# A causal attention and gated FFN kernel: another order and other transfers at its start

## Chip, cores, metric

The kernel runs on one core of a Trainium2 chip. The metric is the time of one execution on the device in microseconds. Runs of one kernel are compared by their median; beside them stands one execution that was recorded by the hardware profiler, from which all durations of single instructions come.

## What is computed

Eight batches of eight heads, 576 positions, head width 64, in float32; then a gated feed-forward block over all 4608 rows of width 512. Cut to what matters:

```python
scores = (q @ k.T) / sqrt(64)                  # per batch and head
cum    = cumsum(max(s, 0), axis=-1)
bias   = -(cum[:, None] - cum[None, :])
scores = where(causal, -1e9, scores + minimum(bias, 0))
attn   = softmax(scores)
x      = concat_heads(attn @ v)                # 4608 x 512
out    = (silu(x @ w_gate) * (x @ w_val)) @ w_out
```

## The kernel before

The kernel schedules every instruction by hand: the order in which the program calls its helpers is the order of each engine's queue. Heads are taken in groups of four ("batches" of the program, `hb`); batch 0 holds heads 0 to 3, batch 1 heads 4 to 7, and together they are the first of the eight batches of the reference. In a group, head `hh` belongs to row half `r = hh // 2` and column half `e = hh % 2`.

**The operand tiles.** `KQ[i][r]` holds, for the groups of parity `i`, 128 partitions: 64 carry the transposed k and q of two heads, side by side in the columns, and of the other 64 four carry the bias terms; the rest are zero. For `r = 0` the bias terms are in partitions 64 to 67. A score piece (`score_piece`, matmuls L373) multiplies a 128-column block of the k side with columns of the q side; the bias comes out of the same product, since the four extra rows hold the running sum of s, split into a high and a low bf16 part, and constants. Heads of the first batch add the causal mask by a matmul with the tile `lower` (L367). ScalarE takes the exponential of each piece (L383) and gives the PSUM bank back. A head has four pieces.

**The running sum.** VectorE scales s (L240), sums it in one scan (L241), rounds the sum to bf16 (L244), subtracts to get the low part (L245) and copies both parts (L246) in the tile `HL`. For head 0 the rows are made on chip: `pick` multiplies `HL` with a selecting matrix (L914; the high part is `lo` = 0, the low part `lo` = 1), and `picked_row` scales and shifts the product from PSUM into `KQ[0][0]`, for one side on ScalarE (L925), for the other on VectorE (L929). All other heads get their rows by `aug`, a DMA from `HL` for each head (L188).

**k and q of batch 0** are loaded in four quarters (k and q, row halves 0 and 1) by SP, in float32; ScalarE casts the first two to bf16 (L268), GpSimd the other two (L270). TensorE transposes each (`row_half`, L315) and the result is copied out of PSUM into `KQ` by `pe_out` (L328 on ScalarE, L330 on VectorE).

**Batch 1** is loaded by GpSimd's queue (L145). VectorE casts k (L260), GpSimd casts q (L260). `half_batch` transposes a whole k or q on TensorE (L301) and copies out row half 0; the copies of row half 1 come later, after the scores of head 3, and only they give the PSUM banks back (L330; four copies for each row half).

**V** is loaded in five chunks by GpSimd's queue (L162), cast by GpSimd (four) and VectorE (the fifth), L173. `init_vt` sets the column of ones beside each head's V and zeroes the padding.

**PSUM** has eight banks. `take` gives the bank that was released longest ago in the order of the program, so a bank's next user waits for its last reader, whichever engine that is.

**The order at the start.** TensorE first runs 32 matmuls on the identity (`keep_warm`, L900) while the first loads are under way. Then come row half 0 of batch 0, the picks, head 0 (with row half 1 transposed in between), head 1, the transposes of k 1, the first two pieces of head 2, the transposes of q 1, the rest of head 2, head 3, heads 4 and 5, and after them the first values products (`values(0, 1)`, L410). The feed-forward block (L643, L749 and others) begins some microseconds later and then runs interleaved with the attention of the next batches to the end.

Of the kernel before, what the change touches and what calls it, by code (L numbers as in the profile page):

```python
# [13 lines left out]
BF16 = mybir.dt.bfloat16  # L14
AF = mybir.ActivationFunctionType
ALU = mybir.AluOpType
# [3 lines left out]
def kernel(  # L20
# [89 lines left out]
    r_m = first.tile([128, 1], FP32)  # L110
    PTP = {0: first, "bufs": 7}
    lower = first.tile([128, 512], BF16)

    with tc.manual_schedule():
        loaded = {}
# [19 lines left out]
        def view(b, w):  # L135
            return bank[b][:, 0:w]
# [4 lines left out]
        def load_one(hb, name, rs=(0, NR), eng=nc.sync):  # L141
            b, g = divmod(hb, 2)
            if rs[0] == 0:
                loaded[name, hb] = raw.tile([128, NR, J, D], FP32, tag="raw" + name, name="raw" + name)
            eng.dma_start(  # L145
                loaded[name, hb][:, rs[0] : rs[1], :, :].rearrange("x r j d -> x r (j d)"),
                SRC[name][0][b, g * HB + 2 * rs[0] : g * HB + 2 * rs[1], :, :].rearrange(
                    "(r e) (p j) d -> (e p) r (j d)", e=2, j=J
                ),
            )  # L150

# [42 lines left out]
        def init_vt(i):  # L194
            nc.gpsimd.memset(VT[i][:, :, :, D : D + 1], 1.0)
            nc.gpsimd.memset(VT[i][64:128, 4, :, 0:D], 0.0)

        for r in range(NR):
            load_one(0, "k", (r, r + 1))
            load_one(0, "q", (r, r + 1))  # L200

        nc.vector.memset(warm, 0.0)
        nc.vector.memset(one_s, 1.0)
        nc.scalar.activation(warm, warm, AF.Exp)
        nc.vector.memset(sel, 0.0)
        nc.vector.memset(HL[:, 0:2, 0, :].bitcast(FP32), ONES2)
        nc.vector.memset(HL[:, 2:4, 1, :].bitcast(FP32), NEGS2)
        make_identity(nc, ident)
        nc.gpsimd.memset(lower, 0.0)
        nc.gpsimd.affine_select(  # L210
            lower, lower, pattern=[[0, 4], [1, 128]],
            compare_op=ALU.is_ge, fill=nc.gpsimd.to_reg(MASKED), base=0, channel_multiplier=-1,
        )
# [8 lines left out]
        nc.vector.memset(aug_rows(0, 0)[:, :, S // 2 :], 0.0)  # L222

        def pads(i):
            for r in range(2):
                nc.gpsimd.memset(KQ[i][r][64 * r : 64 * r + 64, :, NR * S :], 0.0)

        for i in range(2):
            rows = aug_rows(i, 1)
# [1 line left out]
                rows.rearrange("p a n -> p (a n)"),  # L231
                one_s[0:64, 0:1].to_broadcast([64, NR * S + 64]), 0.0,
            )
        nc.gpsimd.memset(aug_rows(1, 0), 0.0)
        pads(0)
        pads(1)
        for nm in ("k", "q"):
            load_one(1, nm, eng=nc.gpsimd)

        nc.vector.tensor_scalar(s_sb, s_sb, 0.0, 8.0, ALU.max, ALU.mult)  # L240
        nc.vector.tensor_tensor_scan(  # L241
            c8, one_s[0:BH, 0:1].to_broadcast([BH, S]), s_sb, 0.0, ALU.mult, ALU.add
        )
        nc.vector.tensor_copy(HL[:, 0, 1, :], c8)  # L244
        nc.vector.tensor_sub(HL[:, 1, 1, :], c8, HL[:, 0, 1, :])  # L245
        nc.vector.tensor_copy(HL[:, 2:4, 0, :], HL[:, 0:2, 1, :])  # L246

        SP4 = [nc.sync] * 4
        GP4 = [nc.gpsimd] * 4

        cts = {}

        def cast_one(hb, name, eng):
            cts[name, hb] = cp.tile([128, J, NR, D], BF16, tag="c" + name, bufs=2, name="c" + name)
            dst = cts[name, hb].rearrange("x j r d -> x r j d")
            src_t = loaded[name, hb]
            if eng is nc.scalar:
                nc.scalar.copy(dst, src_t)
            else:
                eng.tensor_copy(dst, src_t)  # L260

        def cast_half(hb, name, r, eng):
            if r == 0:
                cts[name, hb] = cp.tile([128, J, NR, D], BF16, tag="c" + name, bufs=2, name="c" + name)
            dst = cts[name, hb][:, :, r, :]
            src_t = loaded[name, hb][:, r, :, :]
            if eng is nc.scalar:
                nc.scalar.copy(dst, src_t)  # L268
            else:
                eng.tensor_copy(dst, src_t)  # L270
# [35 lines left out]
        def pe_transpose_half(hb, name, g, r):  # L306
            j0, j1 = JG[g]
            if r == 0:
                bs = EARLY[name][g]
                ps = view16(bs, (j1 - j0) * 128).rearrange("p (j x) -> p j x", x=128)  # L310
                tps[name, g] = [ps, bs, 2]
            ps = tps[name, g][0]
            ct = cts[name, hb]
            for j in range(j0, j1):
                nc.tensor.transpose(  # L315
                    ps[64 * r : 64 * r + 64, j - j0, :], ct[:, j, r, :], ident
                )

        def pe_out(hb, name, g, r, eng):
# [32 lines left out]
        def score_piece(bh, ci):  # L352
            hb, hh = divmod(bh, HB)
            masked = bh < H
            if ci == 0:
                pts[bh] = PTP[0].tile(
                    [128, PTW], BF16, tag="pt", bufs=PTP["bufs"], name="pt"
                )
            pt = pts[bh]
            r, e = divmod(hh, 2)  # L360
            T = KQ[hb % 2][r]
            bs = take()
            n = sum(hi - lo for _, lo, hi in CHUNKS[ci])
            sc = view(bs, n)
            masked_here = masked and ci in (0, 3)
            if masked_here:
                nc.tensor.matmul(  # L367
                    sc, ident, lower[:, 0:n], start=True, stop=False, skip_group_check=True
                )
            o = 0  # L370
            for (tj, lo, hi) in CHUNKS[ci]:
                w = hi - lo
                nc.tensor.matmul(  # L373
                    sc[:, o : o + w],
                    T[:, 1, e * S + 128 * tj : e * S + 128 * (tj + 1)],
                    T[:, 0, e * S + lo : e * S + hi],
                    start=not masked_here,
                    stop=True,
                    skip_group_check=masked_here,
                )  # L380
                o += w
            c0 = CHUNK_PT[ci]
            nc.scalar.activation(pt[:, c0 : c0 + n], sc, AF.Exp, scale=0.125)  # L383
# [513 lines left out]

        def keep_warm(n, b):
            for _ in range(n):
                nc.tensor.matmul(view(b, 128), ident, ident, start=True, stop=True)  # L900

        def row_half(nm, r):
            for g in range(2):
# [3 lines left out]
            for g in range(2):  # L907
                pe_out(0, nm, g, r, engs[g])

        def pick(side):  # L910
            b = PICK[side]
            for lo in range(2):
                for c0, c1 in ((0, 512), (512, S)):
                    nc.tensor.matmul(  # L914
                        banks[:, b + c0 // 512, 0 : c1 - c0], sel[:, lo, :],
                        HL[:, lo, 1, c0:c1], start=(lo == 0), stop=(lo == 1),
                        skip_group_check=True,
                    )

        def picked_row(side):  # L920
            b = PICK[side]
# [24 lines left out]
                av_piece(h, range(NCH))  # L946
                av_out(h)

        keep_warm(32, 7)
        cast_half(0, "k", 0, nc.scalar)  # L950
        cast_half(0, "q", 0, nc.scalar)
        aug(0, SP4, range(1, HB))
        aug(1, SP4)
        row_half("k", 0)
        row_out("k", 0, nc.scalar, nc.scalar)
        cast_half(0, "k", 1, nc.gpsimd)
        cast_half(0, "q", 1, nc.gpsimd)
        load_v(0, range(5), nc.gpsimd)
        row_half("q", 0)
        pick(1)  # L960
        pick(0)
        pe_out(0, "q", 0, 0, nc.scalar)
        pe_out(0, "q", 1, 0, nc.vector)
        picked_row(1)
        picked_row(0)
        row_half("k", 1)
        score_piece(0, 0)
        score_piece(0, 1)
        row_half("q", 1)
        row_out("k", 1, nc.vector, nc.vector)  # L970
        cast_one(1, "k", nc.vector)
        row_out("q", 1, nc.vector, nc.vector)
        score_piece(0, 2)
        score_piece(0, 3)
# [146 lines left out]
```

## Time and profile before

| | |
|---|---|
| median of 3 runs | 374.61 us (373.37 to 375.18) |
| profiled execution | 373.92 us, its span 372.0 us |
| granted TensorE clock, mean | 0.998 |
| TensorE busy | 363.2 us (98%) in 3288 matmuls |
| VectorE busy | 291.1 us (78%) |
| ScalarE busy | 239.9 us (65%) |
| GpSimd busy | 212.4 us (57%) |
| DMA | 64.21 MB, mean 173 GB/s |

The span runs from the first to the last instruction that the profiler recorded; the execution is longer by what lies around it. "Busy" does not count instructions that issue a DMA. In the lists of the trace, lines of the form "start, duration, engine, line, operation, output<-input, shapes, count" merge neighbouring instructions of one line, and a bracket tells how long the engine had been idle and what ended that. "DVE" is VectorE, "ACT" ScalarE, "PE" TensorE, "POOL" GpSimd; "PEld" is TensorE's weight load.

### The profile page before, as it was taken

What the parts mean: (1) busy time and instruction counts of PE and PEld (TensorE: products, weight loads), DVE (VectorE), ACT (ScalarE), POOL (GpSimd) and SP (SyncE); (2) the same over time, 40 slices, a digit from 0 to 9 for tenths busy, and PEclk for the clock granted to TensorE, in tenths of its full rate; (3) what the DMA queues carried; (4) which work ended last, traced back from release to release, by engine and by line L of the source; (5) the groups of instructions that cost most, each with busy time, mean ns of one, the idle gap of its engine ahead of it and who ended that gap; (6) DMA issues with size and microseconds to landing.
All of it is one profiled execution on the core that took longest, in us unless ns stands there. A gap on an engine that the chain in (4) does not pass through costs nothing.

```text
span 372.0 us, 8786 instructions
## 1 busy us (share of the span) xinstructions
PE 363.2 (98%) x3288; PEld 230.3 (62%) x3288; DVE 291.1 (78%) x585; ACT 239.9 (65%) x470; POOL 212.4 (57%) x325
## 2 busy tenths in 40 slices
PE   7899999999999999999999999999999999999996
PEld 6684556655555557855685558655865585476465
DVE  8978776377985899589967897699868867975984
ACT  8877776778886967688757875786565523323321
POOL 8983556955266547594749464955675516315320
PEclk9999999999999999999999999999999999999999
DMA  7999999799879996996789484994142113002003
GB/s 238 220 254 259 215 272 257 239 299 227 252 172 307 199 268 181 162 285 217 214 179 263 160 185 157 265 210 114 40 121 62 35 30 118 0 3 86 28 0 113
DMA packets 97133, 64.21 MB, mean 173 GB/s; under 512 B 77228, under 2 KB 82724, under 8 KB 97092
## 3 DMA queue, kind: packets, MB, share of 16 engines
q1 hardware_dynamic: 84964, 41.46, 46.9%
q0 software_dynamic: 12128, 22.21, 22.7%
q8 instruction: 25, 0.41, 0.5%
q14 instruction: 16, 0.13, 0.1%
HBM read 37.90 MB, written 19.86 MB: 155 GB/s over the span
## 4 chain that ended last, share of the span: by engine, by line
PE 83%; DVE 10%; DMA 2%; ACT 2%; issue 2%; POOL 1%; DVEq 0%; ACTq 0%
PE banks L643 43%; PE banks L749 17%; PE banks L373 9%; PE banks L410 7%; PE banks L700 5%; DVE kq L330 3%; DMA pk<-ks 2%; DVE pp L666 2%; DVE ht L677 1%; DVE kq L288 1%; ACT th L664 1%; POOL vt L173 1%; ACT pt L383 1%; PE banks L459 1%; PE banks L301 0%
## 5 line engine op out<-in xcount | busy, mean ns | idle before, releaser
L383 ACT ACTIVATE pt<-banks 128x512 bf16<-128x512 f32 (+1 forms) x256 | 120.4, 511 | 29.8 <-PE banks L373 17.1
L643 PE MATMUL banks<-XT,wg 128*128 128x512 bf16 x432 | 111.4, 379 | 0.4 <-DVE pp L666 0.3
L643 PE MATMUL banks<-XT,wv 128*128 128x512 bf16 x432 | 110.9, 379 | 0.1
L664 ACT ACTIVATE th<-banks 128x512 bf16<-128x512 f32 x108 | 64.7, 599 | 56.3 <-PE banks L643 51.4
L666 DVE SCALAR_TENSOR_TENSOR pp<-th,banks 128x512 bf16<-128x512 bf16 x108 | 73.7, 682 | 18.3 <-ACT th L664 18.0
L677 DVE SCALAR_TENSOR_TENSOR ht<-pp,banks 128x512 bf16<-128x512 bf16 x108 | 74.1, 687 | 10.3
L373 PE MATMUL banks<-kq 128*128 128x128 bf16 (+4 forms) x576 | 76.4, 240 | 0.8 <-DVE kq L330 0.3
L686 POOL TENSOR_TENSOR ht<-ht 128x512 bf16<-128x512 bf16 x35 | 40.4, 1154 | 53.3 <-DVE su L684 53.2
L373 PEld LDWEIGHTS <-kq 128*128 128x128 bf16 x576 | 46.1, 98 | 30.7 <-issue 2.4
L643 PEld LDWEIGHTS <-wv 128*128 128x128 bf16 x432 | 38.4, 98 | 36.2 <-issue 0.2
L643 PEld LDWEIGHTS <-wg 128*128 128x128 bf16 x432 | 38.4, 98 | 34.1 <-issue 0.7
L410 PEld LDWEIGHTS <-pt 128*128 128x128 bf16 x960 | 41.8, 98 | 17.7 <-issue 0.7
L388 POOL TENSOR_SCALAR_AFFINE_SELECT pt<-pt 128x512 bf16<-128x512 bf16 x56 | 36.6, 653 | 25.9 <-ACT pt L383 21.7
L410 PE MATMUL banks<-vt,pt 128*128 128x65 bf16 x960 | 46.8, 194 | 0.5 <-DVE ot L427 0.4
L444 POOL DMA_DIRECT2D xs<-ot x24 | 21.7, 904 | 30.4 <-DVE ot L427 28.0
L749 PEld LDWEIGHTS <-ht 128*128 128x128 bf16 x336 | 31.2, 98 | 4.3
L427 DVE TENSOR_TENSOR ot<-banks,rc 128x320 bf16<-128x320 f32 x64 | 31.5, 492 | 2.2
L188 POOL DMA_DIRECT2D kq<-HL x48 | 29.2, 610 | 0.0
L700 PE MATMUL banks<-wo,ht 128*128 128x512 bf16 x96 | 25.8, 379 | 0.0
L749 PEld LDWEIGHTS <-su 128*128 128x128 bf16 x252 | 23.6, 98 | 3.3
L814 POOL TENSOR_TENSOR ysb<-ysb 128x512 f32<-128x512 f32 x12 | 15.2, 1269 | 15.3 <-DVE ysb L808 15.3
L749 PE MATMUL banks<-WS,ht 128*128 128x256 bf16 x168 | 22.9, 273 | 0.0
(101 smaller groups left out, 377.2 us busy)
## 6 DMA issues: line engine op xcount, KB each, us to landing
out_dram<-ysb POOLq DMA_DIRECT2D x32, 256.0 KB, 4.0
rawv<-in_v_dram SPq DMA_DIRECT2D x28, 256.0 KB
rawk<-in_k_dram SPq DMA_DIRECT2D x12, 576.0 KB
rawq<-in_q_dram SPq DMA_DIRECT2D x12, 576.0 KB
xs<-ot POOLq DMA_DIRECT2D x24, 160.0 KB, 3.7
ks<-ck SPq DMA_DIRECT2D x11, 288.0 KB
qs<-cq SPq DMA_DIRECT2D x11, 288.0 KB
rawk<-in_k_dram POOLq DMA_DIRECT2D x3, 576.0 KB, 6.0
```

Of the source, the lines that this page charges most:

```text
L373: nc.tensor.matmul(sc[:, o : o + w], T[:, 1, e * S + 128 * tj : e * S + 128 * (tj + 1)], T[:, 0, e * S + lo : e * S + hi], start=not maske ...
L383: nc.scalar.activation(pt[:, c0 : c0 + n], sc, AF.Exp, scale=0.125)
L388: nc.gpsimd.affine_select(pt[:, 1088:1600], pt[:, 1088:1600], pattern=[[0, 4], [1, 128]], compare_op=ALU.is_ge, fill=zreg, base=0, channel ...
L410: nc.tensor.matmul(av[:, bi * (D + 1) : (bi + 1) * (D + 1)], pt[:, c0 : c0 + 128], VT[b % 2][:, tj, h, :], start=(tj == 0), stop=(tj == bi),)
L427: nc.vector.tensor_mul(ot[:, :, e * D : (e + 1) * D], av3[:, :, 0:D], rc[:, :, None].to_broadcast([128, NCH, D]),)
L643: nc.tensor.matmul(view(bs, TT), w[:, c, f0 : f0 + 128], xt[:, c, :], start=(c == 0), stop=(c == 3),)
L664: nc.scalar.activation(th, pg, AF.Tanh, scale=0.5)
L666: nc.vector.scalar_tensor_tensor(pp, in0=th, scalar=1.0, in1=pg, op0=ALU.add, op1=ALU.mult)
L677: nc.vector.scalar_tensor_tensor(hp[:, 2 * k2 : 2 * k2 + 2, :].rearrange("p a n -> p (a n)"), in0=pp, scalar=0.5, in1=pv, op0=ALU.mult, op ...
L686: (nc.vector if ft == NFT - 1 else nc.gpsimd).tensor_sub(hp[:, 1:3, :], hp[:, 1:4:2, :], hp[:, 0:3:2, :])
L700: nc.tensor.matmul(view(pys[ts_], DM), hps[ft // 2][:, 2 * (ft % 2) + half, c0 : c0 + 128], WO[j][:, ft % WKO, :], start=(ft == 0), stop=( ...
L749: nc.tensor.matmul(ps, lhs(p), rhs(p), start=(first and p == 0), stop=(last and p == NP - 1), skip_group_check=True,)
```

## The change

All of it lies in the first 20 us, but for the number of partitions in the scores of row half 0, which holds for all batches.

1. The four quarters of k and q of batch 0 are loaded by GpSimd's queue, which casts them to bf16 on the way (`load_first`); the four casts on ScalarE and GpSimd are gone, `cast_half` with them. The identity is made ahead of these loads, the mask tile `lower` behind them. k of batch 1 is loaded next, q of batch 1 only after `lower`, the zeroed pads and V's ones (`init_vt(0)`, which moves to this place).
2. The scan of s, its rounding and the subtraction run in two halves of 288 columns; ScalarE rounds the first half. The copy of both parts (L246) becomes `second_copy`, behind the bias rows of head 0.
3. Head 1's rows are written by three DMAs from `HL`, the low and high part straight from where they are made (`aug_one`); heads 2 and 3 get theirs as before, after `second_copy`.
4. Scores of row half 0 read 68 partitions instead of 128. The zeroing of the other partitions (L222 on VectorE, L234 on GpSimd) is gone.
5. The picks run high parts first, then low parts.
6. q of batch 1 is cast by VectorE instead of GpSimd.
7. The transposes of k 1 come after the first two pieces of head 2, those of q 1 after its last two.
8. `keep_warm` multiplies a zeroed tile `idle` instead of the identity, 31 times instead of 32, and 18 more such matmuls stand between head 0's third and fourth piece, on a bank of their own.

The diff's core:

```diff
+        def load_first(name, r):
+            ...
+            nc.gpsimd.dma_start(
+                firsts[name][:, r].rearrange("x j d -> x (j d)"),
+                SRC[name][0][0, 2 * r : 2 * r + 2, :, :].rearrange(
+                    "e (p j) d -> (e p) (j d)", j=J
+                ),
+            )
+        make_identity(nc, ident)
         for r in range(NR):
-            load_one(0, "k", (r, r + 1))
-            load_one(0, "q", (r, r + 1))
+            load_first("k", r)
+            load_first("q", r)
+        load_one(1, "k", eng=nc.gpsimd)
         nc.vector.memset(one_s, 1.0)
+        nc.vector.memset(idle, 0.0)
...
-        nc.vector.memset(aug_rows(0, 0)[:, :, S // 2 :], 0.0)
...
-        nc.gpsimd.memset(aug_rows(1, 0), 0.0)
         pads(0)
+        init_vt(0)
         pads(1)
-        for nm in ("k", "q"):
-            load_one(1, nm, eng=nc.gpsimd)
+        load_one(1, "q", eng=nc.gpsimd)
...
-        nc.vector.tensor_tensor_scan(
-            c8, one_s[0:BH, 0:1].to_broadcast([BH, S]), s_sb, 0.0, ALU.mult, ALU.add
-        )
-        nc.vector.tensor_copy(HL[:, 0, 1, :], c8)
-        nc.vector.tensor_sub(HL[:, 1, 1, :], c8, HL[:, 0, 1, :])
-        nc.vector.tensor_copy(HL[:, 2:4, 0, :], HL[:, 0:2, 1, :])
+        for c0 in (0, SH):
+            nc.vector.tensor_tensor_scan(
+                c8[:, c0 : c0 + SH], one_s[0:BH, 0:1].to_broadcast([BH, SH]),
+                s_sb[:, c0 : c0 + SH], c8[:, c0 - 1 : c0] if c0 else 0.0, ALU.mult, ALU.add,
+            )
+        nc.scalar.copy(HL[:, 0, 1, 0:SH], c8[:, 0:SH])
+        nc.vector.tensor_copy(HL[:, 0, 1, SH:], c8[:, SH:])
+        for c0 in (0, SH):
+            c = slice(c0, c0 + SH)
+            nc.vector.tensor_sub(HL[:, 1, 1, c], c8[:, c], HL[:, 0, 1, c])
+        def aug_one():
+            rows = KQ[0][0][:, :, S : 2 * S]
+            nc.sync.dma_start(rows[66:68, 1, :], HL[1:2, 2:4, 1, :])
+            nc.sync.dma_start(rows[64:66, :, :], HL[1:2, 0:2, :, :])
+            nc.sync.dma_start(rows[66:68, 0, :], HL[1:2, 0:2, 1, :])
...
-            T = KQ[hb % 2][r]
+            T = KQ[hb % 2][r][0 : 68 if r == 0 else 128]
...
-        keep_warm(32, 7)
-        cast_half(0, "k", 0, nc.scalar)
-        cast_half(0, "q", 0, nc.scalar)
-        aug(0, SP4, range(1, HB))
-        aug(1, SP4)
+        keep_warm(31, 7)
+        aug_one()
+        load_v(0, range(5), nc.gpsimd)
         row_half("k", 0)
         row_out("k", 0, nc.scalar, nc.scalar)
...
+        second_copy()
+        aug(0, SP4, range(2, HB))
+        aug(1, SP4)
         row_half("k", 1)
         score_piece(0, 0)
         score_piece(0, 1)
         row_half("q", 1)
         row_out("k", 1, nc.vector, nc.vector)
+        row_out("q", 1, nc.vector, nc.vector)
         cast_one(1, "k", nc.vector)
-        row_out("q", 1, nc.vector, nc.vector)
+        cast_one(1, "q", nc.vector)
         score_piece(0, 2)
+        b = take()
+        for _ in range(18):
+            nc.tensor.matmul(view(b, 128), idle, idle, start=True, stop=True)
+        give(b)
         score_piece(0, 3)
-        cast_one(1, "q", nc.gpsimd)
         w_load("g", 0)
-        init_vt(0)
...
         scores(1)
-        half_batch("k")
         score_piece(2, 0)
         score_piece(2, 1)
-        half_batch("q")
+        half_batch("k")
         score_piece(2, 2)
         score_piece(2, 3)
+        half_batch("q")
         scores(3)
```

More of the change, by code (lines that the diff above doesn't have):

```diff
@@ L112 @@
     lower = first.tile([128, 512], BF16)
+    idle = first.tile([128, 128], BF16)
     with tc.manual_schedule():
@@ L148, in load_one @@
                     "(r e) (p j) d -> (e p) r (j d)", e=2, j=J
+                ),
+            )
+        cts = {}
+        firsts = {}
+        def load_first(name, r):
+            if r == 0:
+                cts[name, 0] = cp.tile(
+                    [128, J, NR, D], BF16, tag="c" + name, bufs=2, name="c" + name
+                )
+                firsts[name] = cts[name, 0].rearrange("x j r d -> x (j r d)").rearrange(
+                    "x (r j d) -> x r j d", r=NR, j=J
+                )
+            nc.gpsimd.dma_start(
+                firsts[name][:, r].rearrange("x j d -> x (j d)"),
+                SRC[name][0][0, 2 * r : 2 * r + 2, :, :].rearrange(
+                    "e (p j) d -> (e p) (j d)", j=J
                 ),
@@ L207 @@
         nc.vector.memset(HL[:, 2:4, 1, :].bitcast(FP32), NEGS2)
[L208 to L212, printed above, removed]
-        )
         for lo in range(2):
@@ L221 @@
         nc.vector.tensor_scalar_mul(r_m[up], r_q[up], -1.0)
-        nc.vector.memset(aug_rows(0, 0)[:, :, S // 2 :], 0.0)
+        nc.gpsimd.memset(lower, 0.0)
+        nc.gpsimd.affine_select(
+            lower, lower, pattern=[[0, 4], [1, 128]],
+            compare_op=ALU.is_ge, fill=nc.gpsimd.to_reg(MASKED), base=0, channel_multiplier=-1,
+        )
         def pads(i):
             for r in range(2):
-                nc.gpsimd.memset(KQ[i][r][64 * r : 64 * r + 64, :, NR * S :], 0.0)
+                nc.gpsimd.memset(KQ[i][r][64 * r :, 1, NR * S :], 0.0)
         for i in range(2):
@@ L233, with second_copy @@
             )
-        nc.gpsimd.memset(aug_rows(1, 0), 0.0)
         pads(0)
+        init_vt(0)
         pads(1)
-        for nm in ("k", "q"):
-            load_one(1, nm, eng=nc.gpsimd)
+        load_one(1, "q", eng=nc.gpsimd)
+        SH = S // 2
         nc.vector.tensor_scalar(s_sb, s_sb, 0.0, 8.0, ALU.max, ALU.mult)
-        nc.vector.tensor_tensor_scan(
-            c8, one_s[0:BH, 0:1].to_broadcast([BH, S]), s_sb, 0.0, ALU.mult, ALU.add
-        )
-        nc.vector.tensor_copy(HL[:, 0, 1, :], c8)
-        nc.vector.tensor_sub(HL[:, 1, 1, :], c8, HL[:, 0, 1, :])
-        nc.vector.tensor_copy(HL[:, 2:4, 0, :], HL[:, 0:2, 1, :])
+        for c0 in (0, SH):
+            nc.vector.tensor_tensor_scan(
+                c8[:, c0 : c0 + SH], one_s[0:BH, 0:1].to_broadcast([BH, SH]),
+                s_sb[:, c0 : c0 + SH], c8[:, c0 - 1 : c0] if c0 else 0.0, ALU.mult, ALU.add,
+            )
+        nc.scalar.copy(HL[:, 0, 1, 0:SH], c8[:, 0:SH])
[3 more added lines that the diff above has]
+            nc.vector.tensor_sub(HL[:, 1, 1, c], c8[:, c], HL[:, 0, 1, c])
+        def second_copy():
+            nc.vector.tensor_copy(HL[:, 2:4, 0, :], HL[:, 0:2, 1, :])
+        def aug_one():
[3 more added lines that the diff above has]
+            nc.sync.dma_start(rows[66:68, 0, :], HL[1:2, 0:2, 1, :])
         SP4 = [nc.sync] * 4
         GP4 = [nc.gpsimd] * 4
-        cts = {}
         def cast_one(hb, name, eng):
@@ L256, in cast_one @@
             src_t = loaded[name, hb]
[L257 to L266, printed above, removed]
             if eng is nc.scalar:
@@ L312, in pe_transpose_half @@
             ps = tps[name, g][0]
-            ct = cts[name, hb]
             for j in range(j0, j1):
                 nc.tensor.transpose(
-                    ps[64 * r : 64 * r + 64, j - j0, :], ct[:, j, r, :], ident
+                    ps[64 * r : 64 * r + 64, j - j0, :], firsts[name][:, r, j, :], ident
                 )
@@ L899, in keep_warm @@
             for _ in range(n):
-                nc.tensor.matmul(view(b, 128), ident, ident, start=True, stop=True)
+                nc.tensor.matmul(view(b, 128), idle, idle, start=True, stop=True)
         def row_half(nm, r):
@@ L908, in row_out, with pick @@
                 pe_out(0, nm, g, r, engs[g])
-        def pick(side):
+        def pick(side, lo):
             b = PICK[side]
[L912 to L918, printed above, removed]
+            for c0, c1 in ((0, 512), (512, S)):
+                nc.tensor.matmul(
+                    banks[:, b + c0 // 512, 0 : c1 - c0], sel[:, lo, :],
+                    HL[:, lo, 1, c0:c1], start=(lo == 0), stop=(lo == 1),
+                    skip_group_check=True,
+                )
         def picked_row(side):
@@ L947, in values @@
                 av_out(h)
-        keep_warm(32, 7)
-        cast_half(0, "k", 0, nc.scalar)
-        cast_half(0, "q", 0, nc.scalar)
-        aug(0, SP4, range(1, HB))
-        aug(1, SP4)
+        keep_warm(31, 7)
+        aug_one()
+        load_v(0, range(5), nc.gpsimd)
         row_half("k", 0)
         row_out("k", 0, nc.scalar, nc.scalar)
-        cast_half(0, "k", 1, nc.gpsimd)
-        cast_half(0, "q", 1, nc.gpsimd)
-        load_v(0, range(5), nc.gpsimd)
         row_half("q", 0)
[L960 to L963, printed above, removed]
+        row_out("q", 0, nc.scalar, nc.vector)
+        for lo in range(2):
+            for kq in (1, 0):
+                pick(kq, lo)
         picked_row(1)
         picked_row(0)
+        second_copy()
+        aug(0, SP4, range(2, HB))
+        aug(1, SP4)
         row_half("k", 1)
@@ L970 @@
         row_out("k", 1, nc.vector, nc.vector)
+        row_out("q", 1, nc.vector, nc.vector)
         cast_one(1, "k", nc.vector)
-        row_out("q", 1, nc.vector, nc.vector)
+        cast_one(1, "q", nc.vector)
         score_piece(0, 2)
+        b = take()
+        for _ in range(18):
+            nc.tensor.matmul(view(b, 128), idle, idle, start=True, stop=True)
+        give(b)
         score_piece(0, 3)
-        cast_one(1, "q", nc.gpsimd)
         w_load("g", 0)
-        init_vt(0)
         for c in range(3):
```

## The prediction, made blind

> **What bounds the kernel now.** I read the page's busy shares first: TensorE is busy for 363.2 of 372.0 us, so a change of the start can only shift the moment from which TensorE is never idle again. Then the table of windows, to find that moment:
>
> ```profile
> core 0: us, PE busy (x) PEld busy (x) DVE busy (x) ACT busy (x) POOL busy (x), PEclk, DMA share, GB/s
> 16.00:20.00 4.00, 3.48 (x53) 2.62 (x53) 3.59 (x7) 4.00 (x12) 4.00 (x8) 1.00 1.12 204
> 20.00:24.00 4.00, 4.00 (x93) 3.50 (x90) 3.04 (x10) 3.62 (x10) 3.53 (x5) 1.00 1.02 320
> 24.00:28.00 4.00, 4.00 (x64) 2.94 (x61) 2.73 (x8) 2.01 (x5) 3.10 (x5) 1.00 1.27 196
> 28.00:32.00 4.00, 4.00 (x33) 2.23 (x30) 3.58 (x6) 3.60 (x7) 1.50 (x3) 1.00 1.27 192
> ```
>
> TensorE is full (4.00 of 4.00) from 20 us on and has holes before. What releases it at 19 us stands in the chain of waits of the first 20 us:
>
> ```profile
> 3.11 0.59 DVE kq L222
> ...
> 3.73 0.56 DVE s_sb L240
> ...
> 4.32 1.36 DVE c L241
> ...
> 6.97 0.80 DVE HL L246
> 7.77 0.61 DVE kq L330
> ...
> 10.73 0.76 DVE ck L260
> ...
> 15.96 2.83 DVE kq L330 x4
> 18.79 0.04 issue
> 18.83 0.19 PE banks L367
> ```
>
> From 3.1 to 18.8 us the chain is VectorE alone, back to back. Its last four steps copy batch 1's transposes out (L330) and give back the PSUM bank that head 5's last score piece (L367) takes. Behind them comes V's fifth chunk, without which the first values product can't end. Third, the timeline of the engines:
>
> ```profile
> 18.81 0.55 DVE L173 CAST vt<-rawv 64x512 bf16<-64x512 f32 x1
> 9.80 3.46 ACT L383 ACTIVATE pt<-banks 128x512 bf16<-128x512 f32 x8 [0.98 <-PE banks L373]
> 4.68 0.67 ACT L268 CAST ck<-rawk 128x576 bf16<-128x576 f32 x1 [0.16 <-DMA rawk<-in_k_dram]
> 12.65 1.16 POOL L260 CAST cq<-rawq 128x1152 bf16<-128x1152 f32 x1
> ```
>
> So I take one gate: the end of that V cast, 18.81 + 0.55 = 19.36 us. ScalarE is the near second: its first exponential starts at 9.80, its 32 end at 24.12 (22.43 + 1.69), and values of heads 6 and 7, which need them, start there (24.15). What the change does to the time is what it does to the gate, as long as ScalarE's row does not end later.
>
> **The change, along VectorE's queue.** Everything ahead of the V cast is in VectorE's order, so each instruction counts.
>
> Start: the zeroing at L222 (0.59) goes; a small memset (`idle`, 128x128 bf16) comes, near `sel`'s 0.17. After L221 ends at 3.03 VectorE would be ready at about 3.2. The scaling of s (L240) waited for nothing at 3.73, so the trace only says that s had landed by then. SP issues s first in both kernels, at 0.81; the first quarter of k, issued at 1.45, was used at 4.68, that is 3.2 later, and s is half as large. I take 3.35 for s (bounds 3.2 and 3.73): 0.38 gained.
>
> Scan and split: one-column instructions (L219 to L221) take 0.15, so I call 0.15 the fixed part of each. Scan, 1.35: two halves of 0.15 + 0.60 = 0.75, sum 1.50, +0.15. The rounding copy, 0.45: VectorE keeps the second half, 0.30, -0.15; ScalarE's half ends under VectorE's second scan. The subtraction, 0.75: two of 0.45, +0.15, of which the overlap of neighbours (L330's rows start 0.73 apart though they take up to 0.83) hides about 0.1. Net +0.05 with an issue gap. HL's low part is ready at about 6.93 - 0.38 + 0.05 = 6.6.
>
> Picks: q 0's second copy (0.71) fills 6.6 to 7.3. The four `lo`=1 picks start at 6.7; all eight took 1.15, so four take about 0.6, and the bias rows (L929, 0.89) start at about 7.4 where plain order gives 7.3: +0.1.
>
> Second copy: the 0.80 us copy L246 moves behind the bias rows but stays ahead of the rest, so its length still counts. Its row is too long for its shape. The same shape elsewhere:
>
> ```profile
> L288 DVE COPY kq<-pq x22: 441/457/948, 82.2 to 265.8; 64x1152 bf16<-64x1152 bf16 x22
> ```
>
> The columns are minimum, median and longest ns. At 6.97 GpSimd was casting k and q (0.92 and 0.89); those casts go. I take 0.50 (bounds 0.44 and 0.95): -0.30.
>
> Cast of q 1: 1.16 on GpSimd at 12.65, under VectorE's work, becomes 0.76 on VectorE in front of all eight L330 copies of batch 1, as k 1's did (10.73 to L330's start at 11.53): +0.80. Queued behind it are those copies, the V cast, and through the banks TensorE.
>
> Moved and free: head 2's pieces ahead of k 1's transposes change TensorE's order, which has idle time before 18.8 (3.48 of 4.00 even in the last window) and needs batch 1's transposes only when VectorE has ended its casts. The 18 fillers, at 0.056 apiece (transposes at L315 run 9 in 0.69 with the drain) 1.0 us, 2.0 at the keep-warm's 0.11, stand in the same idle time; they do hold back head 0's fourth piece and head 1, so ScalarE loses about that much of what it gains below. Head 1's rows by three SP transfers: the first waits for constants only, the other two leave SP from 6.6 on, 0.6 to 0.8 apiece (L188), where the one they replace left at 7.80. Heads 2 and 3 now wait for the second copy (8.7) instead of queueing behind head 1 (7.80 and one issue, 8.6), batch 1's four follow as now: nothing on SP is later by more than 0.2, and batch 1's rows are needed only at 16 us. V's ones set early cost GpSimd 0.32 + 0.52 before the loads of q 1 and V instead of 14.50.
>
> Sum so far: -0.38 + 0.05 + 0.10 - 0.30 + 0.80 = +0.27 us at the gate.
>
> Loads: k 0 and q 0 go from SP to GpSimd's queue, behind the identity (ends 1.38). Issues there take 0.55 (`out_dram<-ysb`, one row per partition) to 0.91 (L145), say 0.7. The landing has no row for an idle queue: SP's quarter took 3.2 to its use, GpSimd's loads beside other traffic:
>
> ```profile
> rawk<-in_k_dram POOLq DMA_DIRECT2D x1, 576.0 KB, 5.3
> rawv<-in_v_dram POOLq DMA_DIRECT2D x1, 256.0 KB, 4.5
> ```
>
> So k 0 is there between 4.6 and 6.7, q 0 0.7 later. Near 4.6, since at 1.4 us the DMA engines are empty as for SP's load (0.43 share in 0 to 4 us, 0.92 and more after): I take 5.0, q 0 5.7. TensorE's transposes of both end at about 6.4, picks then end at 7.5 instead of 7.3: +0.1 more. The Trainium skill ("DMA: Bandwidth & Descriptors", section "Latency and other measured facts") says that a load from GpSimd's queue starts about 0.4 us later than one from SP's, and its fit (section "Anatomy of one DMA") is 2.0 us and bytes over 436 GB/s, 2.7 us here; by that, k 0 lands at an estimated 4.1 and this term is nothing, while the POOL rows above lie at 4.5 and more.
>
> q 1: four quarter loads (2.8), k 1 (0.8), `lower` (0.52 + 0.63), pads and V's ones (0.2 a memset, 0.32, 0.52) put its issue near 8.0 (5.75 now). 4.5 to 5.3 later is 12.5 to 13.3; less if its queue is empty. VectorE asks for it at 10.73 + 0.80 + 1.50 (q 0's row-1 copies now come first) - 0.43 (the first four terms and k 0's 0.1) = about 12.6: a wait of 0 to 0.7, I take 0.2.
>
> Gate: +0.27 + 0.1 + 0.2 = **+0.6 us**. Bounds: s at 3.2 (-0.15), second copy 0.44 (-0.06), no lateness (-0.3) give +0.1; s at 3.73 (+0.38), copy 0.95 (+0.45), q 1's 0.7 (+0.5) give +1.9. A gain is excluded as long as the V cast is the gate, since the cast of q 1 alone outweighs what VectorE can save. V's loads are issued at 8.25 now and about 8.8 then; GpSimd is rid of three casts (0.92, 0.89, 1.16) and the 1.11 zeroing, so its V casts, which end at 18.46, are no later.
>
> ScalarE: loses two casts (1.34) and gains half a copy (about 0.4): its bias rows end at 8.82 - 0.9 = about 7.9 to 8.3, the first exponential starts near 8.7, 1.1 earlier, and the fillers take most of that back. It is not late.
>
> The profiled execution took 373.92 (span 372.0 and 1.9 around it); the runs' median, 374.61, is 0.69 above. 373.92 + 0.6 = 374.5 as a profiled time, 374.61 + 0.6 = **375.2** as a median.
>
> **Rivals.** (a) The first loads decide, slower. If k 0 lands as GpSimd's k 1 did, at 1.4 + 5.3 = 6.7, TensorE stands still from the fillers' end (1.2 + 31 x 0.107 = 4.5) to 6.7, q 0 lands at 7.4, transposes and picks (0.69 + 1.15) end at 9.2 instead of 7.4: +1.8, with the +0.27 and q 1's 0.2 some +2.3: 376.9. If TensorE's clock then is still the early one (keep-warm matmuls 0.107 apart, transposes 0.056), 18 transposes and the picks add up to 1.9 more. It decides from k 0 at 5.6 on. For it: every GpSimd load in the trace took 4.5 or more. Against: all met a busy queue. The Trainium skill ("TensorE: Matmul & The Clock Gate", section "What's actually happening") lets the clock fall only after an idle window of 3.4 us; by it a pause of 2.2 us costs no clock.
>
> (b) ScalarE decides, faster. Were the exponentials and not VectorE's copies the last to end, the gate would move with the first exponential, 1.1 us less, at most 1.4: 373.2 to 373.5. Against: TensorE's wait at 18.83 ends with L330, not with an exponential, and VectorE's queue only grows.
>
> (c) The edits don't reach the end: VectorE's gain and the cast cancel, 374.6.
>
> (d) 68-row weight loads cost more: 288 of L373's 576. Nearest row, 64-row loads at L914: 0.106 against 0.098; 288 x 0.008 = 2.3 if nothing hid it, but the loads overlap matmuls: 376.9, unlikely.
>
> **How the numbers follow.** Forecast (+0.1 to +1.3) 0.45, (a) 0.28, (b) 0.12, (c) 0.10, (d) 0.05. 0.5% is 1.9 us, about what a measurement can tell from no change. Slower by more: (a) and (d) nearly whole, 0.31. Faster by more: (b) at its end with a low measurement, 0.09. The rest, 0.60, is within. Range: from (b)'s near end, 373.3, to (a), 377.2.
>
> **What would show it.** Right: VectorE one unbroken row from about 3.4 to the V cast, which ends near 20.0; the second copy at 0.5; the cast of q 1 near 12.6 with a short wait for its DMA; first exponential near 8.7. Wrong: k 0's transposes after 5.6 (a); TensorE before 19 us waiting for an exponential and the V cast unimportant (b); L373's matmuls with longer means (d).

## The result, and the profile after

The changed kernel took 376.99 us (median of 7 runs, 376.02 to 377.74), the kernel before 374.5 beside it. The ratio is 1.0068, its 95% interval 1.0045 to 1.0091: some 2.5 us slower, and the interval leaves out no change. The profiled execution took 376.98, its span 374.9 (before 372.0). Lines have moved: L350 is the copy that was L330, L393 the score matmul (L373), L387 the mask (L367), L322 the transposes of batch 1 (L301), L948 the bias rows (L929), L273 the second copy (L246), L207 the rows by DMA (L188), L335 the transposes of batch 0 (L315), L933 the picks (L914). The ratios leave out executions far above the rest of their kernel (one of a2 took 1353 us).

First the table of windows; columns as before:

```profile
12.00:16.00 4.00, 2.39 (x31) 1.61 (x29) 2.75 (x5) 2.59 (x7) 2.84 (x4) 1.00 1.03 239
16.00:20.00 4.00, 3.46 (x40) 2.40 (x39) 3.97 (x7) 3.63 (x10) 2.96 (x5) 1.00 1.17 196
20.00:24.00 4.00, 3.37 (x66) 2.65 (x66) 3.21 (x7) 3.04 (x8) 3.91 (x6) 1.00 1.03 319
24.00:28.00 4.00, 4.00 (x100) 3.61 (x97) 3.34 (x11) 3.17 (x8) 3.21 (x4) 1.00 1.18 192
```

TensorE is full in the windows from 24 us on; before it was full from 20. The moment has shifted, as the prediction said it would, but by more. By how much stands in VectorE's timeline (start, duration, engine, line; a bracket is idle time ahead of it):

```profile
3.57 0.64 DVE L260 TENSOR_SCALAR s_sb<-s_sb 64x576 f32<-64x576 f32 x1 [0.65 <-DMA s_sb<-in_s_dram]
...
5.88 0.56 DVE L267 CAST HL<-c 64x288 bf16<-64x288 f32 x1
...
8.24 0.89 DVE L948 TENSOR_SCALAR kq<-banks,r_q,r_k 64x576 bf16<-64x576 f32 x1 [0.35 <-PE banks L933]
9.15 0.78 DVE L273 COPY HL<-HL 64x1152 bf16<-64x1152 bf16 x1
9.96 2.82 DVE L350 COPY kq<-banks 64x640 bf16<-64x640 bf16 x4
12.81 0.76 DVE L291 CAST ck<-rawk 128x1152 bf16<-128x1152 f32 x1
13.49 0.94 DVE L291 CAST cq<-rawq 128x1152 bf16<-128x1152 f32 x1
15.65 5.63 DVE L350 COPY kq<-banks 64x640 bf16<-64x640 bf16 x8 [1.22 <-PE banks L322]
21.31 0.65 DVE L192 CAST vt<-rawv 64x512 bf16<-64x512 f32 x1
```

The gate, the end of V's fifth chunk, is at 21.31 + 0.65 = 21.96: 2.60 later than before's 19.36. The row is not unbroken: behind the cast of q 1 VectorE stands for 1.22 us, because TensorE has not transposed k 1 yet. Why it has not is in TensorE's timeline and in the chain of waits:

```profile
4.99 1.17 PE L335 MATMUL banks<-ident,ck 128*64 128x128 bf16 x9 [0.39 <-DMA ck<-in_k_dram]
5.95 1.16 PE L335 MATMUL banks<-ident,cq 128*64 128x128 bf16 x9
...
14.72 0.62 PE L393 MATMUL banks<-kq 128*128 128x128 bf16 x6 [1.51 <-DMA kq<-HL]
15.17 0.67 PE L322 MATMUL banks<-ident,ck 128*128 128x128 bf16 x9
```

```profile
1.52 3.43 DMA ck<-in_k_dram
...
4.99 2.12 PE banks L335 x18
7.11 1.10 PE banks L933 x8
...
8.24 0.90 DVE kq L948
...
9.15 0.79 DVE HL L273
...
9.96 4.71 DMA kq<-HL
...
14.72 0.62 PE banks L393 x6
15.34 0.50 PE banks L322 x9
...
18.46 2.83 DVE kq L350 x4
```

Before, this chain was VectorE alone from 3.1 to 18.8 us. Now it begins with the load of k 0, the first 18 transposes and the picks, and a transfer of 4.71 us stands in it. That transfer is head 2's bias row, which SP issues at 9.96, when the second copy has ended. Head 2's first piece waits for it, and behind that piece stand, by the new order, the transposes of k 1. Before, they came first and began at 12.41, as soon as they had banks:

```profile
12.41 0.44 PE L301 MATMUL banks<-ident,ck 128*128 128x128 bf16 x5 [0.49 <-DVE kq L330]
```

The loss is made at the start and kept: TensorE's first output matmul begins at 146.40, before at 144.12, 2.28 later, and the last group of them at 369.97, before at 367.52, 2.45 later.

### The profile page after: what moved, and what is told of

Its sections match the earlier page's. It is cut to its first block, busy times and chain, and to the rows that moved or that the text cites. A ratio compares the mean times of both kernels' runs of the same rounds, so it can differ in the third digit from the quotient of the medians.

```text
span 374.9 us, 8822 instructions
## 1 busy us (share of the span) xinstructions
PE 365.3 (97%) x3305; PEld 231.6 (62%) x3305; DVE 292.5 (78%) x588; ACT 239.6 (64%) x469; POOL 211.4 (56%) x325
## 4 chain that ended last, share of the span: by engine, by line
PE 87%; DVE 6%; DMA 2%; ACT 1%; issue 1%; POOL 1%; DVEq 0%; POOLq 0%; ACTq 0%
PE banks L663 45%; PE banks L769 17%; PE banks L393 10%; PE banks L430 7%; PE banks L720 5%; DVE kq L350 2%; DVE pp L686 1%; DMA kq<-HL 1%; DVE ht L697 1%; DMA ck<-in_k_dram 1%; PE banks L322 1%; POOL vt L192 1%; PE banks L335 1%; PE banks L479 1%; ACT th L684 0%
## 5 line engine op out<-in xcount | busy, mean ns | idle before, releaser
L393 PE MATMUL banks<-kq 68*128 68x128 bf16 (+9 forms) x576 | 76.5, 240 | 2.8 <-DMA kq<-HL 1.5
L393 PEld LDWEIGHTS <-kq 68*128 68x128 bf16 (+1 forms) x576 | 46.0, 98 | 33.1 <-issue 2.8
L207 POOL DMA_DIRECT2D kq<-HL x48 | 28.9, 605 | 0.0
L413 POOL TENSOR_SCALAR_AFFINE_SELECT pt<-pt 128x64 bf16<-128x64 bf16 x56 | 14.9, 267 | 16.5 <-ACT pt L403 16.3
```

The source lines that it names most:

```text
L393: nc.tensor.matmul(sc[:, o : o + w], T[:, 1, e * S + 128 * tj : e * S + 128 * (tj + 1)], T[:, 0, e * S + lo : e * S + hi], start=not maske ...
```

## The experiments

Each kernel's ratio goes against runs of the kernel before on the same chip; "gate" is the end of V's fifth cast in its profiled execution (before 19.36, after 21.96). Prefix a is an edit of the changed kernel, b of the kernel before. The ratio is not the quotient of the two medians, which lies up to 0.2 points away; so differences of that size between two kernels are not read.

**a1: the old order of head 2 and k 1, all else as changed.**

```diff
-        score_piece(2, 0)
-        score_piece(2, 1)
         half_batch("k")
+        score_piece(2, 0)
+        score_piece(2, 1)
+        half_batch("q")
         score_piece(2, 2)
         score_piece(2, 3)
-        half_batch("q")
```

> The changed kernel with the transposes of k 1 and q 1 put back to their old places (k 1 ahead of head 2's first piece, q 1 after its second). Theory A: VectorE's 1.22 us of waiting at 14.4 us comes from head 2's bias row, which leaves SP at 9.96 and is used at 14.67; TensorE stands before head 2's first piece with k 1's transposes queued behind it. With k 1 ahead, VectorE copies it out as soon as its two casts end (about 14.4): the V cast ends 1.2 us earlier, at 20.75 instead of 21.96, and the time is 375.8 against 377.0 of the changed kernel (ratio to before 1.0035). Rival W: it is the work added to VectorE (the cast of q 1, the longer copies) that costs, and another wait takes the place of this one: V cast at 21.9, 377.0 (1.0067).

Measured 375.86, ratio 1.0024 (0.9997 to 1.0051). VectorE no longer stands; its timeline:

```profile
13.87 5.63 DVE L350 COPY kq<-banks 64x640 bf16<-64x640 bf16 x8
19.53 0.49 DVE L192 CAST vt<-rawv 64x512 bf16<-64x512 f32 x1
```

Gate 20.02, 1.94 earlier than after and 0.66 later than before. Of the 1.94, the wait is 1.22. The other 0.7 comes from steps that a1 does not edit: the bias rows begin at 7.95 for 8.24, the second copy takes 0.45 for 0.78, the V cast 0.49 for 0.65. So the order explains about half of the 2.60 at the gate. The timed runs fall from 1.0068 to 1.0024; the two intervals just overlap, and they do not say which of these parts is gone. No other wait took the place of this one, as rival W had it; nearest is V's fourth chunk, whose cast on GpSimd ends at 19.73.

**a2: the order kept, the row earlier.** The second copy goes right behind the subtractions, and the rows of heads 2 and up leave SP from 8.68 instead of 9.96.

```diff
+        second_copy()
         aug_one()
+        aug(0, SP4, range(2, HB))
+        aug(1, SP4)
...
-        second_copy()
-        aug(0, SP4, range(2, HB))
-        aug(1, SP4)
```

> The changed kernel with the second copy put back right behind the subtractions, so that the rows of heads 2 and 3 and of batch 1 can leave SP from about 8.6 instead of 9.96. Theory A: head 2's row is there by about 12, TensorE's wait of 1.5 us and VectorE's of 1.22 fall, and the copy also fills VectorE's idle 0.35 us ahead of the bias rows: the V cast ends at about 20.3, 375.3 (1.002); the first exponential is about 0.4 later than 9.60. Rival W: only the idle 0.35 to 0.5 us is won: 21.5, 376.5 (1.0054).

Measured 375.75, 1.0031 (1.0006 to 1.0055), gate 19.63 + 0.42 = 20.05. TensorE's timeline shows head 2's piece without a wait, and VectorE's is left with 0.21:

```profile
13.05 0.60 PE L393 MATMUL banks<-kq 128*128 128x128 bf16 x6
13.49 0.67 PE L322 MATMUL banks<-ident,ck 128*128 128x128 bf16 x9
```

So the wait goes by either end of the dependence: with the piece behind the transposes, or with the row ahead of the piece. That settles the cause of the wait.

**a3: q 1 cast by GpSimd again, the row still late.**

```diff
-        cast_one(1, "q", nc.vector)
...
+        cast_one(1, "q", nc.gpsimd)
         w_load("g", 0)
```

> The changed kernel with q 1 cast by GpSimd again, behind its loads of V. Theory A: 0.94 us leave VectorE, but head 2's row still comes at 14.67 and k 1's transposes behind it, so VectorE only waits longer (from about 13.5 to 15.65): V cast at 21.96, 377.0 (1.0067), no change. Rival W: all of it is won, V cast at 21.0, 376.0 (1.004).

Measured 377.36, 1.0076 (1.0049 to 1.0103). VectorE's 0.94 us of cast is gone and its wait has grown:

```profile
15.21 5.63 DVE L350 COPY kq<-banks 64x640 bf16<-64x640 bf16 x8 [2.24 <-PE banks L322]
```

The second copy here took 0.45 and SP issued the row at 9.31, but it lasted 4.92 and was there at 14.23; the gate is 20.87 + 0.71 = 21.58. As long as the row holds everything up, the cast on VectorE lies in its shadow.

**b1: the kernel before with only the new order.**

> The kernel before with only the order of the change: head 2's first two pieces ahead of k 1's transposes, its last two ahead of q 1's. Theory A: head 2's row is there at 11.4 (issued 8.67), the order alone costs next to nothing: 374.5 (1.000). Rival: the order costs by itself, because head 2's first pieces wait for the PSUM banks of q 0's copies (12.3 and 13.0) and k 1's transposes come after them: k 1's copies start at 13.4 instead of 13.03, 374.9 (1.001).

Measured 375.59, 1.0031 (1.0002 to 1.0060), gate 21.03: more than expected. The row is not what is late here. TensorE's timeline, then VectorE's:

```profile
13.32 0.38 PE L367 MATMUL banks<-lower,ident 128*128 128x512 bf16 x1 [1.39 <-DVE kq L330]
13.96 0.60 PE L373 MATMUL banks<-kq 128*128 128x128 bf16 x6 [0.26 <-DVE kq L330]
14.39 0.67 PE L301 MATMUL banks<-ident,ck 128*128 128x128 bf16 x9
```

```profile
10.74 1.67 DVE L260 CAST ck<-rawk 128x1152 bf16<-128x1152 f32 x1
12.44 1.46 DVE L330 COPY kq<-banks 64x640 bf16<-64x640 bf16 x2
14.95 5.64 DVE L330 COPY kq<-banks 64x640 bf16<-64x640 bf16 x8 [1.04 <-PE banks L301]
```

Head 2 needs q 0's second half in `KQ`, and before copies that behind the cast of k 1. With the new order k 1's transposes wait for those copies too. The wait of 1.04 is the order's own price; the other 0.6 is what is left of a longer cast of k 1 (1.67 here, 0.76 before) after a shorter V cast (0.42 for 0.55) and a slightly shorter row of copies (7.13 for 7.28). Theory A, that the order alone is nearly free, was wrong. The changed kernel escapes this wait by copying q 0 first, and runs into the row.

**a4: the changed kernel without the 18 fillers.**

```diff
-        b = take()
-        for _ in range(18):
-            nc.tensor.matmul(view(b, 128), idle, idle, start=True, stop=True)
-        give(b)
```

> The changed kernel without the 18 filler matmuls between head 0's third and fourth piece. Theory A (head 2's row, then VectorE's queue): the fillers stand in TensorE's idle time, the V cast still ends near 21.96; 377.0 against 377.0 of the changed kernel (ratio to before 1.0067), the exponentials of heads 0 and 1 about 1 us earlier. Rival F: the fillers hold ScalarE back and that is part of the loss: up to 1 us less, 376.0.

Measured 378.71, 1.0107 (1.0070 to 1.0144): slower, where none or a gain was expected. The windows of its profile show one reason (the first figure behind the five engines is the granted clock):

```profile
12.00:16.00 4.00, 1.74 (x19) 1.06 (x18) 2.72 (x5) 2.22 (x7) 2.74 (x4) 1.00 1.06 228
16.00:20.00 4.00, 3.70 (x27) 2.72 (x28) 3.80 (x6) 2.41 (x7) 2.84 (x5) 0.57 1.16 192
```

After a window with 1.74 us of work TensorE got the low clock, from 16.27 to 19.68, with the longest pause ahead of it 2.11 us (for head 2's row). The nine transposes of q 1 took 1.14 instead of 0.67, and the gate is 22.08. This execution also holds a separate wait for a transfer at 239 to 248 us. Its output matmuls tell the two apart: against before they are 3.07 later at 222 us, where the changed kernel's are 2.37 later, and 5.29 later at 261 us. So in this profile the start without fillers costs 0.70, the later wait 2.22. How much of the 1.7 us of the timed runs is the clock's is not settled.

**a8: the fillers out, but with the old order (a1 without fillers)**, to see whether the clock falls by the fillers alone.

> The changed kernel with k 1's and q 1's transposes in their old places and without the 18 fillers. Theory C: in the changed kernel the fillers only pay because TensorE stands still for head 2's row (12.9 to 14.7) and its clock falls for 3.4 us without them; with k 1 first there is no such pause, the clock stays, and the time is that with k 1 first alone, 375.9 (1.0024), or up to 0.3 less. Rival F: TensorE's start has too little work without the fillers in any case, the clock falls again: 377.4 (1.006).

Measured 376.30, 1.0035 (1.0010 to 1.0060), gate 20.30. In the profile the clock held, with a pause of 1.63 the longest. The other executions say more. In a4's profile one low stretch of 3.41 us makes a mean clock of 0.995. At 0.995 or below lie 5 of a4's 6 executions and 7 of a8's 12, but only 2 of 12 in a1 and 2 of 7 in the changed kernel. So without the fillers the clock falls often with the old order too: that is rival F, and theory C rested on one profile. Where in those executions the clock falls was not recorded. In the profile, head 2's row was in the chain here too, 5.18 us long, and held VectorE for 0.25.

**b2: the kernel before with q 1 cast by VectorE.**

```diff
         row_out("q", 1, nc.vector, nc.vector)
+        cast_one(1, "q", nc.vector)
...
-        cast_one(1, "q", nc.gpsimd)
```

> The kernel before with only the cast of q 1 moved to VectorE, behind q 0's second-half copies. If VectorE's queue is the limit of the kernel before, the cast counts in full: 0.76 and an issue gap, V cast's end at 20.15 instead of 19.36, 375.05 (1.002). Rival S (ScalarE is the limit): no change, 374.3.

Measured 375.87, 1.0024 (0.9994 to 1.0054), gate 20.47, +1.11; VectorE's timeline:

```profile
13.04 0.98 DVE L260 CAST cq<-rawq 128x1152 bf16<-128x1152 f32 x1
14.06 5.64 DVE L330 COPY kq<-banks 64x640 bf16<-64x640 bf16 x8
19.73 0.74 DVE L173 CAST vt<-rawv 64x512 bf16<-64x512 f32 x1
```

A cast put in VectorE's row shifts everything behind it by its own length (1.02 from start to start), and the V cast was 0.19 longer. By this profile the gate's reading holds, and ScalarE, the rival, does not decide; the timed interval just includes no change.

**a5, a6, a7: taking back more.** a5 joins a1 and a3; a6 also issues q 1's load right behind k 1's; a7 also casts k 1 ahead of q 0's second-half copies, as before.

```diff
         load_one(1, "k", eng=nc.gpsimd)
+        load_one(1, "q", eng=nc.gpsimd)       # a6, a7; taken out behind pads(1)
...
+        cast_one(1, "k", nc.vector)           # a7
         row_out("q", 1, nc.vector, nc.vector)
-        cast_one(1, "k", nc.vector)           # a7
```

> k 1's and q 1's transposes in their old places and q 1 cast by GpSimd again, everything else as changed. With the wait for head 2's row out of the way, VectorE's queue should be the limit, and the cast that brought nothing while the wait stood (377.4 against 377.0) should now pay: VectorE 0.9 us shorter than with the order alone (V cast's end 20.02), 19.2, time 375.0 (1.001). Rival V: V's fourth chunk, cast by GpSimd at 19.1 to 19.7 when the order alone was put back, is next in line and comes later still behind the cast of q 1: the first values product ends at 20 or later, 375.9 (1.0035).

> As the one before, and q 1 is loaded right behind k 1, as before the change, ahead of the mask tile, the pads and V's ones. The DMA engines, a quarter busy from 8 to 9 us in the changed kernel, have work then, and V's chunks land up to 1 us earlier. If V's fourth chunk was the limit, this gives the rest: VectorE alone at 19.2, 374.3 to 375.0 (0.9995 to 1.001), 0.5 to 0.9 less than the one before. If VectorE was, nothing changes against the one before, or the mask tile, now later, holds the first score piece back.

> As the kernel with k 1 first, q 1 cast by GpSimd and loaded early, and k 1 is cast ahead of q 0's second-half copies, as before the change. VectorE waited 0.55 us there for k 1's transposes, since their cast was the last thing ahead of them; now TensorE can transpose under q 0's copies. VectorE's queue theory: V cast's end at 19.1 instead of 19.65, 374.1 (0.9995 to 1.0005 of before). If instead the wait moves to the PSUM banks or to q 1's cast on GpSimd, no change: 374.6 (1.0018).

Measured: a5 375.37, 1.0035 (1.0012 to 1.0058), gate 20.38; a6 374.61, 1.0018 (0.9988 to 1.0049), gate 19.65; a7 375.12, 1.0007 (0.9981 to 1.0033), gate 19.82. In a5 VectorE gets rid of the cast and waits instead: 0.55 for k 1's transposes, which follow its cast at once, and 0.31 for those of q 1, held up by head 2's row (4.92) ahead of them; the V cast is longer too, 0.78. With q 1's load earlier (a6) the second wait and the long V cast are gone. VectorE's timeline of a6, then of a7:

```profile
13.53 5.67 DVE L350 COPY kq<-banks 64x640 bf16<-64x640 bf16 x8 [0.55 <-PE banks L322]
19.23 0.42 DVE L192 CAST vt<-rawv 64x512 bf16<-64x512 f32 x1
```

```profile
11.74 1.46 DVE L350 COPY kq<-banks 64x640 bf16<-64x640 bf16 x2
13.73 5.64 DVE L350 COPY kq<-banks 64x640 bf16<-64x640 bf16 x8 [0.53 <-PE banks L322]
```

In a6 the 0.55 is the cast of k 1 coming last ahead of its transposes. a7 cured that, and the same wait came back because the transposes then need the banks that q 0's copies free. Both are as fast as before within some 0.5%, neither is shown to be faster: of the change's other parts no gain is left over that these runs can tell.

**b4: the kernel before with only the cast loads** (k 0, q 0 by GpSimd's queue, the four casts gone; identity first, k 1 next, q 1 last).

> The kernel before with only the loads of the change: identity first, k 0 and q 0 by cast loads on GpSimd's queue, k 1 loaded right behind them, q 1 in its old place behind mask tile and pads; no casts of k 0 and q 0. The second copy runs without GpSimd's casts beside it (0.45 instead of 0.80): V cast's end up to 0.35 earlier, 373.9 (0.999). If the cast loads come too late for the picks, as in the changed kernel where TensorE's transposes ran from 4.99 to 7.1 and the bias rows started at 8.2, this is nothing or up to 0.3 more: 374.6 (1.001).

Measured 375.45, 1.0030 (1.0001 to 1.0059), gate 20.25, where a gain was expected. GpSimd's timeline, then VectorE's:

```profile
8.54 0.74 POOL L145 DMA_DIRECT2D rawq<-in_q_dram  x1
...
13.74 1.14 POOL L276 CAST cq<-rawq 128x1152 bf16<-128x1152 f32 x1
```

```profile
15.50 4.30 DVE L345 COPY kq<-banks 64x640 bf16<-64x640 bf16 x6 [0.88 <-PE banks L317]
```

The bias rows begin at 8.37, for 8.44 before: the start gained next to nothing. What four more issues on GpSimd push back, q 1 and its cast, ends at 14.88, and VectorE waits 0.88 for its transposes. A cast of q 1 on VectorE, as the change has it, takes that wait away, and costs by b2 about as much.

**b3: the kernel before with only the 68-partition scores**, the zeroings taken out with them and the pads beside them (L226) made smaller, as in the change.

```diff
-        nc.vector.memset(aug_rows(0, 0)[:, :, S // 2 :], 0.0)
...
-        nc.gpsimd.memset(aug_rows(1, 0), 0.0)
...
-            T = KQ[hb % 2][r]
+            T = KQ[hb % 2][r][0 : 68 if r == 0 else 128]
```

> The kernel before with only the 68-partition scores and without the two zeroings they save (0.59 on VectorE, 1.11 on GpSimd). VectorE's queue theory: s came at 3.57 where VectorE began at 3.73, so at most 0.16 is won on VectorE; GpSimd's loads of k 1, q 1 and V are 1.1 earlier, off the path: 374.1 to 374.3 (0.999 to 1.000). Rival D: 68-row weight loads are dearer, up to 2.3 us more: 376.5 (1.006).

Measured 376.31, 1.0034 (1.0009 to 1.0058), gate 20.96, again where a gain was expected. The weight loads are not the cost: 97 ns on 68 rows, 98 on 128. Of the 1.60 that the gate is late, 0.98 is the cast of k 1, which took 1.74 here for 0.76 before, as in b1; why is not shown. The bias rows, which begin at 9.04 for 8.44, are the other 0.60. GpSimd, rid of 1.11 us of zeroing, issues k 1 and q 1 earlier (GpSimd's timeline), and the chain of waits then begins with a load that SP issued when it always did:

```profile
3.24 0.91 POOL L145 DMA_DIRECT2D rawk<-in_k_dram  x1
4.14 0.74 POOL L145 DMA_DIRECT2D rawq<-in_q_dram  x1
7.39 0.68 POOL L268 CAST ck<-rawk 128x576 bf16<-128x576 f32 x1 [2.51 <-DMA rawk<-in_k_dram]
```

```profile
2.07 4.41 DMA rawq<-in_q_dram
...
6.50 0.68 ACT cq L266
```

Before, q 0's first half was cast at 5.43; here at 6.50. Nor did VectorE gain by its own zeroing: s landed only at 3.86, where it was there by 3.73 before. The likeliest reading of the 0.60 is that the early loads of batch 1, 576 KB each, share the DMA engines with SP's quarters. No run moved those loads alone, so this reading is argued and not shown.

## Why the prediction was right, and where it was wrong

**The number.** The forecast was +0.6 us and 375.2; measured were 2.60 at the gate and 376.99. That is beyond the forecast's own band (+0.1 to +1.3) and beyond the +1.9 that its sum allowed. The measured time lies inside the stated range only because the range reached up to rival (a), which did not happen as described. That is luck.

**Right.** The gate and its row. By the timed runs the excess and the gate's shift agree to within 0.7 us, but for a4: 2.5 and 2.60 in after, 0.9 and 1.11 in b2, 1.3 and 1.60 in b3. In the profiles the output matmuls at 222 us are shifted by within 0.5 us of the gate in 12 of 13 kernels (a7: 1.16 for 0.46). Behind that, a4, b1, b2 and b3 lose another 0.6 to 2.2 us around 250 us, which the gate does not explain. TensorE is also not quite full to the end, as the prediction read it: from 32 to 40 us it is busy for 7.22 of 8.00 before and 7.23 after. What enters VectorE's queue ahead of the V cast counts in full where no other wait covers it. The casts from the row-1 copies on added 0.68 (predicted 0.80), k 0 was there at 4.95 (5.0), and q 1 was not waited for (0.2). The 68-row loads cost nothing, ScalarE did not decide, and no kernel became faster.

**The step that failed: "Moved and free".** The prediction said that head 2's pieces ahead of k 1's transposes cost nothing, since TensorE has idle time, and that "nothing on SP is later by more than 0.2, and batch 1's rows are needed only at 16 us". It checked batch 1's rows and not head 2's own, and it put no length on that transfer: issued at its 8.7, and taking the 4.7 that it took, the row would have come at an estimated 13.4. It was issued at 9.96, for about 8.6 before, and TensorE could have used it at 13.2 (14.72 less the 1.51 of wait); it came at 14.67. Idle time on TensorE is no cover when the piece put first waits for something else: everything queued behind it waits too. Price: the 1.22 us of VectorE's wait.

**The mis-sized terms**, all on VectorE ahead of that wait, measured against before's rows:

| step | predicted | measured |
|---|---|---|
| s begins (3.73 before) | -0.38 | -0.16 (3.57) |
| scaling, scan, split, to the low part | +0.05 | +0.39 (3.22 before, 3.73 to 6.95; now 3.61, 3.57 to 7.18) |
| picks, with k 0 and q 0 late | +0.20 | +0.39 (1.06 from low part to bias rows, for 1.49 less the copy's 0.82) |
| second copy | -0.30 | +0.10 (0.78; its place adds a gap that overlapped before) |
| casts, q 1's wait | +0.80, +0.20 | +0.68, none |
| wait for k 1's transposes | 0 | +1.22 |
| copies of batch 1, V cast | 0 | -0.02 |
| sum | +0.57 | +2.60 |

Up to the wait the sum is +1.40 instead of +0.57. The second copy took 0.78 in this profile, but 0.45 in six of the eight edits of the changed kernel (a1, a3, a5 to a8) and 0.80 in before, b1 and b2, where GpSimd's casts are beside it: the predicted 0.50 was the usual length, and why after and a4 (0.90) have a long one is open. The rounding copy (0.56 for a predicted 0.30) lay beside GpSimd's making of `lower` (5.18 to 6.27); in a6 and a7, where that begins at 5.91 and 5.92, it took the 0.30. And the first 18 transposes ran at half pace, 1.17 and 1.16 us instead of 0.69 each nine: 0.95 that stood only in rival (a). The picks waited for them; in a1, with full pace, the bias rows begin 0.29 earlier.

**The rivals.** Rival (a) named 376.9, close to what was measured, but by another road: k 0 was in time (4.95; the rival needed 5.6). Its remark on the low clock came true, and the first loads do open the chain, at a price of the picks' +0.39 and not of 1.8. That the number agrees is no support for it. The upper bound of the forecast's sum would have held the +1.40, but not the row on top. ScalarE's first exponential came at 9.60, not near 8.7: its bias rows ended at 8.81, where I had 7.9 to 8.3, because the picks were late. The gate did not wait for it.

## What to carry to other kernels

Before an instruction is moved ahead on an in-order engine, list every operand of it with the time at which it lands, not only those of the work that it overtakes: idle time on the engine covers its length, never its waits, and the whole queue inherits them. A small transfer between on-chip tiles that is issued while large loads fill the DMA engines should be booked at what such transfers take there (here 4.7 to 5.2 us), and a clock that held in one profile is to be checked in the mean clock of all executions. What frees an engine early (b3, b4) is to be followed to what that engine issues next.

## What the runs showed of the hardware that was not expected

- A 9 KB transfer from `HL` to `KQ` (head 2's row) took 4.7 to 5.2 us from issue to use in the four profiles in which it stands in the chain of waits (4.71, 4.92, 4.92, 5.18), with the DMA share at 1.03 while V's loads ran; head 3's took 5.70 in a4. In a1 and a2 the piece found it there 4.45 and 4.37 after its issue.
- The low clock came back in a4 after a pause of 2.11 us, with 1.74 of 4.00 us busy, and stayed for 3.41. The prediction had weighed that a pause of 2.2 costs none. The Trainium skill ("TensorE: Matmul & The Clock Gate", section "What's actually happening") asks for an idle window of about 3.4 us before the clock falls; here 3.41 us with TensorE busy for 1.37 were enough. In a4's trace the clock rises at 6.03, falls at 16.27 and rises at 19.68, steps of 10.24 (three times 3.41) and 3.41. On such a grid, counted from its own rise at 5.36, a8's emptiest step (12.19 to 15.60) has 1.95 us busy, although 11.50 to 14.90 has only 1.25 of 3.40. So it seems to matter where the steps lie, which would fit a clock that falls in some executions of a kernel and not in others; two profiles do not prove it.
- When the clock first rises varies: by the traces at 6.98 us in after and at 4.46 in a1. The first nine transposes ran at 1.17 us in after (from 4.99) and at 0.69 in a1 (from 5.41).
- A low stretch goes with a loss of about a microsecond or more: in a2 the four executions with a mean clock of 0.995 took 376.66 to 377.15, seven at 0.998 and above 374.98 to 375.76.
- The same VectorE instruction differs by up to 2.3 times from one kernel to the next: the second copy 0.45, 0.55, 0.78, 0.90 (a1, a2, after, a4), the cast of k 1 0.76 in before and 1.67 in b1, 1.74 in b3, the V cast 0.42 to 0.78. GpSimd's making of `lower` took 0.63 before and 1.09 beside VectorE's rounding copy. The Trainium skill ("SBUF — State Buffer", section "Who interferes with whom") describes an exclusive lock on ports shared by these two engines, under which copies and casts can block. The pair of longer instructions agrees with it, and so do a6 and a7, where the two no longer overlap and took 0.30 and 0.65; the first subtraction, now beside `lower`, took 0.88 there for 0.44. No run moved that pair alone.
